# The last unit of a six-layer cross network: another product order, finals in pieces, and two quadrants transposed on TensorE in place of DMA

## The chip, the core and the metric

The kernel runs on one core of one Trainium2 chip. The metric is device time in microseconds (us), lower is better. A profile's span is some 2 us shorter than the time of its run. Because the change touches only the last 25 us of 2300, I use one more number throughout, the **tail**: from the end of the last full-size product on TensorE to the end of the span, both read from one profile (spans are given to 0.1 us, so a tail is good to some 0.05 us).

## The reference

```python
# x0: 16384 x 1024, ws: 6 x 1024 x 1024, bs: 6 x 1024, all bf16
x = x0
for l in range(6):
    proj = x @ ws[l] + bs[l]
    x = x0 * proj + x
return x
```

## The kernel before

It takes 1024 rows at a time through all six layers, with the rows along the free dimension. A *unit* is one layer for 1024 rows. In the last unit each matrix product is a Strassen-Winograd product of 2x2 blocks: seven block products P1 to P7, each of four groups (m = 0 to 3) of four 128x128x512 matmuls. They accumulate into eight banks of PSUM: `pA` and `pX`. Four quadrants of the output follow from them: Q (P1, P2), U (P1, P6, P3, P5), V (P1, P6, P7, P5) and W (P1, P6, P7, P4). ScalarE empties the banks, VectorE adds P5 where it is due, multiplies by x0 and adds x (the *finals*).

A hand-written table of ranks gives the order in which operations are issued; each engine and each DMA queue then works in that order. In the last unit the finals write a tile that a DMA transposes to row order, and a second DMA stores it. The part that matters:

```python
ttop("Ua", U[:], U[:], P5s[:], ADD, ...)          # whole quadrants, 128x2048
ttop("Va", V[:], V[:], P5s[:], ADD, ...)
for nm, C, q in (("Q", Q, (0, 0)), ("U", U, (0, 1)), ("V", V, (1, 1)), ("W", W, (1, 0))):
    ...                                            # C *= x0   (W in two halves)
    if not last: ...
    else:
        def fin(...): tt(xfin[...], v4(C[:]), v4(blk(xs, eh, n)), ADD)
        def tr(...):  nc.sync.dma_start_transpose(out=xo[...], in_=xfin[...])
        z = base + {"Q": 40, "U": 41, "V": 42, "W": 43}[nm]
        op(z, tr, ...)
        def st(...):  nc.sync.dma_start(out[...], xo[...])
        op(z + 10, st, ...)                        # all stores rank behind all transposes
```

Of the kernel before, what the change touches and what calls it, by code (L numbers as in the profile page):

```python
# [7 lines left out]

ADD = mybir.AluOpType.add
SUB = mybir.AluOpType.subtract  # L10
MULT = mybir.AluOpType.mult
BF16 = mybir.dt.bfloat16
# [4 lines left out]
def ranks(text):  # L17

    return {w.split("@")[0]: float(w.split("@")[1]) for w in text.split()}
# [25 lines left out]
""")  # L45
RFIRST = {**R0, **ranks("""
T1@-5 c5@-4.5 T2@-4 c6@-3.5 T3@-3 c7@-2.5 c3@-2 T4@-1 2i5@15 2i6@15.1 2i3@15.2 2i7@15.3 5i5@15.4 5i6@15.5 5i3@15.6 5i7@15.7
""")}
SPAN2, SPAN0 = 23.4, 24.2

# [2 lines left out]
def kernel(  # L53
# [7 lines left out]
    nc = tc.nc  # L61
    P = nc.NUM_PARTITIONS
# [3 lines left out]
    KH = KD // 2  # L66
    H = D // 2
    NB = 512
    PR = 2 * NB
    assert D == 1024 and B % PR == 0  # L70
    NPAIR = B // PR
    KQ, HQ, NQ = KH // 2, H // 2, NB // 2
# [3 lines left out]
    const = ctx.enter_context(tc.tile_pool(name="const", bufs=1))  # L76
# [8 lines left out]
    pA = [psum.tile([P, NB], FP32, name=f"pA{i}") for i in range(KH)]  # L85
    pX = [psum.tile([P, NB], FP32, name=f"pX{i}") for i in range(KH)]
    x0Ts = [work.tile([P, 2, KD, NB], BF16, name=f"x0T{i}") for i in range(2)]
    xsts = [work.tile([P, 2, KD, NB], BF16, name=f"xst{i}") for i in range(2)]
# [4 lines left out]
    P1s, P5s, Q, U, V, W = (work.tile([P, KH, NB], BF16, name=f"ev{i}") for i in range(6))  # L93
    isum = [work.tile([P, KH, H], BF16, name=f"isum{i}") for i in range(2)]
    zeros = const.tile([P, NB], BF16, name="zeros")
    LK = L * KD
    b_bf = const.tile([P, LK], BF16, name="b_bf")
    b_all = const.tile([P, LK], FP32, name="b_all")

    def blk(t, dh, n):  # L100
        return t[:, n, dh * KH:(dh + 1) * KH, :]

    def tt(o, a, b, op):
        nc.vector.tensor_tensor(out=o, in0=a, in1=b, op=op)  # L104
# [60 lines left out]
    def op(rank, fn, rd=(), wr=(), weights=()):  # L165
        for k in weights:
            uses_left[k] = uses_left.get(k, 0) + 1
        ops.append((rank, fn, tuple(rd), tuple(wr), tuple(weights)))

    base = 0.0  # L170
    QD = ((0, 0), (0, 1), (1, 0), (1, 1))
    for u, (pr, l) in enumerate(units):
        one, first, last = level1(u), u == 0, u == NU - 1
        rk = RFIRST if first else (R0 if one else R2)
        x0T, xst = x0Ts[pr % 2], xsts[pr % 2]
        xs = x0T if l == 0 else xst
        X0 = {q: f"x0.{pr % 2}.{q[0]}{q[1]}" for q in QD}
        XO = {q: f"xs.{pr % 2}.{q[0]}{q[1]}" for q in QD}
        XI = X0 if l == 0 else XO

        def add(name, fn, rd=(), wr=(), weights=(), rk=rk, base=base, u=u):
            op(base + rk[name], fn, rd, wr, [(u, w) for w in weights])

        def ttop(name, o, a, b, o_, rd, wr, **kw):
            add(name, lambda: tt(o, a, b, o_), rd, wr, **kw)
# [15 lines left out]
        if pr == 0:  # L201
# [13 lines left out]
            for X, s in (("2i", isum[0]), ("5i", isum[1])):  # L215
                a = lambda r, c, X=X, u=u: wt[(u, X[0])][:, r * KQ:(r + 1) * KQ, c * HQ:(c + 1) * HQ]
# [31 lines left out]
        A = [f"A{m}" for m in range(KH)]  # L248
        Xn = [f"X{m}" for m in range(KH)]
        if not one:  # L250
            for X, Bm, src in (("5", T[1][:], "T1"), ("2", B21, XI[1, 0])):
                q = lambda dh, n, Bm=Bm: Bm[:, dh * KQ:(dh + 1) * KQ, n * NQ:(n + 1) * NQ]
# [15 lines left out]
        if not one:  # L268
            for X, Bm, src, a, b, C in (("5", T[1][:], "T1", 0, 1, P5s), ("2", B21, XI[1, 0], 2, 3, Q)):
                q = lambda dh, n, Bm=Bm: Bm[:, dh * KQ:(dh + 1) * KQ, n * NQ:(n + 1) * NQ]  # L270
                c = lambda dh, n, C=C: C[:, dh * KQ:(dh + 1) * KQ, n * NQ:(n + 1) * NQ]
# [48 lines left out]
        allm = lambda s: [f"{s}.{m}" for m in range(KH)]  # L320
        if not one:
            ttop("Q1", Q[:], Q[:], P1s[:], ADD, allm("Q") + allm("P1s"), allm("Q"))
        ttop("Ua", U[:], U[:], P5s[:], ADD, allm("U") + allm("5c"), allm("U"))
        ttop("Va", V[:], V[:], P5s[:], ADD, allm("V") + allm("5c"), allm("V"))
        for nm, C, q in (("Q", Q, (0, 0)), ("U", U, (0, 1)), ("V", V, (1, 1)), ("W", W, (1, 0))):
            if nm == "W":
                for h, g in enumerate("ab"):
                    sl, ms = slice(h * KQ, (h + 1) * KQ), [f"W.{2 * h}", f"W.{2 * h + 1}"]
                    ttop("Wm" + g, C[:, sl], C[:, sl], blk(x0T, *q)[:, sl], MULT, ms + [X0[q]], ms)
            else:  # L330
                ttop(nm + "m", C[:], C[:], blk(x0T, *q), MULT, allm(nm) + [X0[q]], allm(nm))
            if not last:
                ttop(nm + ("a" if nm == "Q" else "x"), blk(xst, *q), C[:], blk(xs, *q), ADD, allm(nm) + [XI[q]], [XO[q]])
            else:
                xfin = xsts[1 - pr % 2][:].rearrange("r n k (j p) -> r (n k j) p", p=P).rearrange(
                    "r (e n j k) p -> r e n j k p", e=2, n=2, j=KH)
                xo = x0Ts[1 - pr % 2][:].rearrange("r n k (j p) -> r (n k j) p", p=P).rearrange(
                    "r (e n j k) p -> r e n j k p", e=2, n=2, j=KH)
                XF = [f"xs.{1 - pr % 2}.{a}{b}" for a, b in QD]
                XT = [f"x0.{1 - pr % 2}.{a}{b}" for a, b in QD]  # L340
                eh, n = q

                def fin(eh=eh, n=n, C=C, xfin=xfin, xs=xs):
                    v4 = lambda a: a.rearrange("r k (j p) -> r k j p", p=P)
                    tt(xfin[:, eh, n].rearrange("r j k p -> r k j p"), v4(C[:]), v4(blk(xs, eh, n)), ADD)
                add(nm + ("a" if nm == "Q" else "x"), fin, allm(nm) + [XI[q]] + XF, [f"xf{eh}{n}"])

                def tr(eh=eh, n=n, xfin=xfin, xo=xo):
                    nc.sync.dma_start_transpose(out=xo[:, eh, n].rearrange("p j k r -> p (j k) r"),
                                                in_=xfin[:, eh, n].rearrange("r j k p -> r (j k p)"))  # L350
                z = base + {"Q": 40, "U": 41, "V": 42, "W": 43}[nm]
                op(z, tr, [f"xf{eh}{n}"] + XT, [f"xt{eh}{n}"])

                def st(eh=eh, n=n, xo=xo, pr=pr):
                    r0 = pr * PR + n * NB
                    nc.sync.dma_start(out[r0:r0 + NB, eh * H:(eh + 1) * H].rearrange("(j p) d -> p j d", p=P),
                                      xo[:, eh, n].rearrange("p j k r -> p j (k r)"))
                op(z + 10, st, [f"xt{eh}{n}"], ["out"])

        nxt = pr + 1  # L360
        if l == (2 if pr == 0 else 0) and nxt < NPAIR:
# [21 lines left out]
    order_ctx = ctx.enter_context(tc.manual_schedule(  # L383
        engines={nc.tensor.engine, nc.scalar.engine, nc.vector.engine, nc.sync.engine, nc.gpsimd.engine}))
    nc.vector.memset(zeros[:], 0.0)
    for i in range(NDUMMY):
        nc.tensor.matmul((pX + pA)[i % (2 * KH)][:], lhsT=zeros[:, 0:P], rhs=zeros[:], start=True, stop=True, skip_group_check=True)

# [80 lines left out]
```

## Time and profile before

| | |
|---|---|
| time, median of 4 runs | 2299.64 us (2299.07 to 2301.93) |
| span of the profile | 2297.4 us |
| last full product ends | 2277.24 us |
| tail | 20.2 us |

The page's table of busy time of the kernel before: busy us, share of the span, number of instructions.

```profile
span 2297.4 us, 34637 instructions
PE 2255.7 (98%) x12674; PEld 1261.1 (55%) x12912; DVE 2079.1 (90%) x2314; ACT 1833.8 (80%) x3223; POOL 20.3 (1%) x41
```

TensorE is busy 98% of the span, so fewer waits before the last product could gain hardly anything. The timeline of the kernel before from there on, engine by engine (start us, duration us, engine, line, operation, output<-inputs, count; SPq is the queue of DMA issues, where a merged line holds several issues and the waits between them):

```profile
2272.76 4.48 PE L190 MATMUL pA<-T,wp 128*128 128x512 bf16 x20
...
2273.97 1.23 DVE L104 TENSOR_TENSOR ev<-ev,ev 128x2048 bf16<-128x2048 bf16 x1 [8.86 <-ACT ev L199]
2275.23 1.23 DVE L104 TENSOR_TENSOR ev<-ev,x0T 128x2048 bf16<-128x2048 bf16 x1
2276.37 1.22 DVE L104 TENSOR_TENSOR ev<-ev,ev 128x2048 bf16<-128x2048 bf16 x1
2277.51 1.29 DVE L104 TENSOR_TENSOR ev<-ev,x0T 128x1024 bf16<-128x1024 bf16 x2
2278.83 2.36 DVE L104 TENSOR_TENSOR xst<-ev,xst 128x2048 bf16<-128x2048 bf16 x2
2281.11 1.22 DVE L104 TENSOR_TENSOR ev<-ev,x0T 128x2048 bf16<-128x2048 bf16 x1
2282.36 1.23 DVE L104 TENSOR_TENSOR xst<-ev,xst 128x2048 bf16<-128x2048 bf16 x1
...
2265.14 23.13 SPq L349 DMA_TRANSPOSE x0T<-xst  x4
2288.36 3.88 SPq L356 DMA_DIRECT2D out_dram<-x0T  x4
```

VectorE idles 8.86 us until ScalarE has emptied all of U's banks, and then has nearly 10 us of finals to do, 6.4 us of them after TensorE has stopped. Q's transpose is issued at 2265.14, but no store is issued before 2288.36, when the fourth transpose has been issued. W's final ends at 2280.05, before U's at 2281.19, yet W's transpose stands last in the queue. The same stretch by windows, kernel before (from:to, length, busy time of each engine, granted clock of TensorE, mean busy share of the DMA engines, which can read a little over 1, GB/s):

```profile
2280.00:2282.00 2.00, 0.00 (x0) 0.00 (x0) 2.00 (x3) 0.00 (x0) 0.00 (x0) 0.50 0.00 0
2282.00:2284.00 2.00, 0.00 (x0) 0.00 (x0) 1.55 (x2) 0.00 (x0) 0.00 (x0) 0.50 0.89 168
2286.00:2288.00 2.00, 0.00 (x0) 0.00 (x0) 0.00 (x0) 0.00 (x0) 0.00 (x0) 0.50 1.14 212
2290.00:2292.00 2.00, 0.00 (x0) 0.00 (x0) 0.00 (x0) 0.00 (x0) 0.00 (x0) 0.50 1.03 350
2294.00:2296.00 2.00, 0.00 (x0) 0.00 (x0) 0.00 (x0) 0.00 (x0) 0.00 (x0) 0.50 0.99 330
2296.00:2297.40 1.40, 0.00 (x0) 0.00 (x0) 0.00 (x0) 0.00 (x0) 0.00 (x0) 0.50 0.00 0
```

From 2282.4 to 2296.0 the DMA engines are full: about 7.4 us for three transposes at some 212 GB/s, then 6.2 us for four stores of 512 KB at some 340 GB/s. Between Q's transpose, which is through by 2269, and 2282 they stand idle. This tail is late DMA work.

### The profile page before, as it was taken

The page shows a single profiled execution, that of the slowest core. Times are in us where ns is not written, and L with a number is a line of the kernel's source. Part 1 is how long each engine was busy: PE and PEld are TensorE (multiplying, and loading weights), DVE is VectorE, ACT ScalarE, POOL GpSimd, SP SyncE. Part 2 cuts the span into 40 slices and gives each one's busy share as a digit, 9 for nine tenths or more (in the row PEclk, how much of TensorE's full clock was granted, in tenths as well). Part 3 has the DMA queues.
Part 4 walks back from the last instruction along what each step waited for, and adds up shares of the span by engine and source line. Part 5 has one row for each costly group of instructions (what it writes and reads, how often), then busy time and mean ns, then how long its engine had stood idle before and what let it go on. Part 6 is the DMA issues. An engine that isn't in the chain of part 4 may idle for free.

```text
span 2297.4 us, 34637 instructions
## 1 busy us (share of the span) xinstructions
PE 2255.7 (98%) x12674; PEld 1261.1 (55%) x12912; DVE 2079.1 (90%) x2314; ACT 1833.8 (80%) x3223; POOL 20.3 (1%) x41
## 2 busy tenths in 40 slices
PE   8999999999999999999999999999999999999996
PEld 3445555555555555555555555555555555555552
DVE  6999999999999999999999999999999999999995
ACT  4668888888888887888888888888888888878884
POOL 1100000000000000000000000000000000000000
PEclk9999999999999999999999999999999999999998
DMA  9669689695977969779697796968869698796953
GB/s 296 237 244 290 226 234 281 203 317 187 252 260 217 305 209 248 263 221 286 214 274 241 227 285 202 291 223 238 281 196 298 206 253 269 209 310 197 276 181 74
DMA packets 627932, 558.06 MB, mean 243 GB/s; under 512 B 401712, under 2 KB 554288, under 8 KB 627760
## 3 DMA queue, kind: packets, MB, share of 16 engines
q1 hardware_dynamic: 622576, 536.95, 78.7%
q0 software_dynamic: 5184, 18.88, 2.1%
q8 instruction: 101, 1.65, 0.3%
q14 instruction: 71, 0.58, 0.1%
HBM read 436.21 MB, written 52.43 MB: 213 GB/s over the span
## 4 chain that ended last, share of the span: by engine, by line
PE 96%; DVE 2%; issue 1%; DMA 1%; SPq 1%; ACT 0%; DVEq 0%; ACTq 0%
PE pA L190 56%; PE pX L288 24%; PE pX L190 16%; DVE ev L104 1%; SPq L390 0%; DMA Lc<-isum 0%; DMA x0T<-in_x_dram 0%; DVE xst L104 0%; DVE wp L104 0%; DVE T L104 0%; ACT ev L199 0%; DVE isum L104 0%; SPq L397 0%; ACT pX L195 0%; DVE ti L104 0%
## 5 line engine op out<-in xcount | busy, mean ns | idle before, releaser
L190 PEld LDWEIGHTS <-wp 128*128 128x128 bf16 x7904 | 771.9, 98 | 851.1 <-issue 10.9
L190 PE MATMUL pA<-T,wp 128*128 128x512 bf16 x4468 | 1049.6, 379 | 7.3
L199 ACT ACTIVATE ev<-pA,b_all 128x512 bf16<-128x512 f32 x1124 | 706.0, 689 | 212.8 <-PE pA L190 166.0
L288 PEld LDWEIGHTS <-wp 128*128 128x128 bf16 x4984 | 486.3, 98 | 158.9 <-issue 16.9
L104 DVE TENSOR_TENSOR ev<-ev,x0T 128x2048 bf16<-128x2048 bf16 (+1 forms) x480 | 482.8, 1007 | 7.7 <-ACT ev L199 1.3
L104 DVE TENSOR_TENSOR xst<-ev,xst 128x2048 bf16<-128x2048 bf16 x320 | 391.1, 1224 | 19.4 <-DVE ev L104 0.5
L288 PE MATMUL pX<-ti,wp 128*128 128x256 bf16 x2848 | 398.1, 272 | 0.6 <-DVE ti L104 0.6
L104 DVE TENSOR_TENSOR ev<-ev,ev 128x2048 bf16<-128x2048 bf16 x281 | 343.6, 1223 | 32.8 <-ACT ev L199 15.3
L199 ACT ACTIVATE ev<-pX,b_all 128x512 bf16<-128x512 f32 x412 | 288.9, 705 | 65.2 <-PE pX L190 46.8
L190 PE MATMUL pX<-xst,wp 128*128 128x512 bf16 x1372 | 337.9, 379 | 2.2 <-DVE xst L104 1.8
L195 ACT COPY pX<-pA 128x512 f32<-128x512 f32 x412 | 256.3, 627 | 63.5 <-PE pA L190 60.8
L190 PE MATMUL pA<-xst,wp 128*128 128x512 bf16 x1203 | 302.1, 379 | 4.0
L195 ACT CAST ev<-pX 128x512 bf16<-128x512 f32 x384 | 224.6, 619 | 38.2 <-ACT ev L199 38.0
L104 DVE TENSOR_TENSOR ev<-iu,ip 128x1024 bf16<-128x1024 bf16 x178 | 122.5, 688 | 121.1 <-ACT iu L195 121.1
L195 ACT COPY pX<-pX 128x512 f32<-128x512 f32 x356 | 208.9, 587 | 8.5
L195 ACT CAST iu<-pX 128x512 bf16<-128x512 f32 x356 | 196.8, 639 | 0.3 <-PE pX L288 0.2
L104 DVE TENSOR_TENSOR T<-xst 128x2048 bf16<-128x2048 bf16 x160 | 194.9, 1218 | 0.5
L104 DVE TENSOR_TENSOR T<-xst,T 128x2048 bf16<-128x2048 bf16 x160 | 194.9, 1218 | 0.4
L288 PE MATMUL pX<-T,wp 128*128 128x256 bf16 x1068 | 160.2, 273 | 0.0
L195 ACT CAST ip<-pX 128x512 bf16<-128x512 f32 x178 | 104.8, 589 | 55.0 <-PE pX L288 55.0
L288 PE MATMUL pX<-xst,wp 128*128 128x256 bf16 x888 | 133.2, 273 | 0.0
L104 DVE TENSOR_TENSOR xst<-ev,x0T 128x2048 bf16<-128x2048 bf16 x64 | 78.2, 1223 | 1.6
(30 smaller groups left out, 614.3 us busy)
## 6 DMA issues: line engine op xcount, KB each, us to landing
wp<-Lc SPq DMA_DIRECT2D x538, 512.0 KB, 4.6
wp<-in_ws_dram SPq DMA_DIRECT2D x288, 512.0 KB, 5.3
out_dram<-x0T SPq DMA_DIRECT2D x30, 1024.0 KB, 10.1
Lc<-wp POOLq DMA_DIRECT2D x24, 512.0 KB, 6.0
Lc<-isum POOLq DMA_DIRECT2D x12, 512.0 KB, 3.6
w<-in_ws_dram SPq DMA_DIRECT2D x6, 512.0 KB, 7.7
out_dram<-x0T SPq DMA_DIRECT2D x4, 512.0 KB, 4.7
x0T<-in_x_dram SPq DMA_TRANSPOSE x34, 7.4
```

The costliest lines, as they stand in the source:

```text
L104: nc.vector.tensor_tensor(out=o, in0=a, in1=b, op=op)
L190: nc.tensor.matmul(bank[:], lhsT=wt[(u, w)][:, k, m * P:(m + 1) * P], rhs=rhs[:, k, :], start=(start and k == 0), stop=(k == KH - 1), skip ...
L195: add(name, lambda: nc.scalar.copy(out=dst, in_=src), rd, wr)
L199: add(name, lambda: nc.scalar.activation(out=dst, in_=src, func=IDENT, bias=b_all[:, c:c + 1], scale=1.0), rd, wr)
L288: nc.tensor.matmul(pX[bank][:, m * NQ:(m + 1) * NQ], lhsT=wv[:, k, m * P:(m + 1) * P], rhs=rhs[:, k, :], start=(start and m == 0 and k == ...
```

## The change

It is to start that DMA work earlier and to take two of the transposes off the DMA engines. In the last unit only:

- The products come in the order P1 P2 P5 P6 P3 P7 P4, each with its four groups in order, so that U and V are complete before the last product, P4, which only W needs.
- U's and V's finals run in halves, W's multiply in quarters.
- Q and U keep their DMA transposes; V and W are transposed on TensorE by matmuls against an identity, into PSUM banks that are free by then. For W, a matmul of x against the identity starts the bank and the one of W accumulates onto it, which is W's last add.
- ScalarE and VectorE copy the banks out; V and W leave in two stores of 256 KB each, the last on ScalarE's queue.

```diff
+RLAST = {**R0, **ranks("""            (a table of ranks for the last unit; cut)
+ ... Ua0@16.6 Um0@17.2 Ux0@17.8 Ua1@18.4 Um1@19 Ux1@19.6 Va0@20.4 Vm0@21 Vx0@21.3 Va1@21.6 Vm1@22.2 Vx1@22.8
+ ... trQ@19 stQ@24 trU@22.5 stU@26 stVa@27 stVb@27.5 stWa@28 stWb@29
+    ident = const.tile([P, P], BF16, name="ident")
...
+            for h in range(2):
+                sl = slice(h * KQ, (h + 1) * KQ)
+                for nm, C, q in (("U", U, (0, 1)), ("V", V, (1, 1))):
+                    ttop(f"{nm}a{h}", C[:, sl], C[:, sl], P5s[:, sl], ADD, ...)
+                    ttop(f"{nm}m{h}", C[:, sl], C[:, sl], blk(x0T, *q)[:, sl], MULT, ...)
+                ttop(f"Vx{h}", V[:, sl], V[:, sl], blk(xs, 1, 1)[:, sl], ADD, ...)
+                ttop(f"Ux{h}", xfin[...][:, sl], v4(U[:])[:, sl], v4(blk(xs, 0, 1))[:, sl], ADD, ...)
+            for m in range(KH):
+                ttop(f"Wm{m}", W[:, m, :], W[:, m, :], blk(x0T, 1, 0)[:, m, :], MULT, ...)
...
+            for nm, C, bank, n in (("V", V, pX, 1), ("W", W, pA, 0)):
+                for m in range(KH):
+                    def part(src, start, stop, bank=bank, m=m):
+                        for j in range(KH):
+                            nc.tensor.matmul(bank[m][:, j * P:(j + 1) * P], lhsT=src[:, m, j * P:(j + 1) * P], rhs=ident[:],
+                                             start=(start and j == 0), stop=stop, skip_group_check=True)
+                    if nm == "W":
+                        add(f"xW.{m}", lambda part=part, xs=xs: part(blk(xs, 1, 0), True, False), ...)
+                    add(f"t{nm}.{m}", lambda part=part, C=C, nm=nm: part(C, nm == "V", True), ...)
+                    # copies: V's four and W's last on ScalarE, W's other three on VectorE
+                add(f"st{nm}a", lambda st2=st2: st2(0, KQ), ...)
+                add(f"st{nm}b", lambda st2=st2, nm=nm: st2(KQ, KH, nc.sync if nm == "V" else nc.scalar), ...)
...
+    make_identity(nc, ident[:])
```

Set against the kernel before, the table of ranks is the same up to the last unit.

More of the change, by code (lines that the diff above doesn't have):

```diff
@@ L7 @@
 from concourse._compat import with_exitstack
+from concourse.masks import make_identity
 ADD = mybir.AluOpType.add
@@ L47 @@
 T1@-5 c5@-4.5 T2@-4 c6@-3.5 T3@-3 c7@-2.5 c3@-2 T4@-1 2i5@15 2i6@15.1 2i3@15.2 2i7@15.3 5i5@15.4 5i6@15.5 5i3@15.6 5i7@15.7
+""")}
+RLAST = {**R0, **ranks("""
+P6.0@10.4 P6.1@11.3 P6.2@12.1 P6.3@13 P3.0@13.9 P3.1@14.7 P3.2@15.6 P3.3@16.4 P7.0@17.3 P7.1@18.2 P7.2@19 P7.3@19.9
+P4.0@20.8 P4.1@21.6 P4.2@22.5 P4.3@23.3
+P2.0@3.5 P2.1@4.4 P2.2@5.2 P2.3@6.1 P5.0@6.9 P5.1@7.8 P5.2@8.7 P5.3@9.5 tV.0@24.4 tV.1@24.6 tV.2@24.8 tV.3@25
+xW.0@25.1 tW.0@25.2 xW.1@25.3 tW.1@25.4 xW.2@25.5 tW.2@25.6 xW.3@25.7 tW.3@26.6
+F1.0@2.8 F1.1@3.2 F1.2@3.7 F1.3@4.1 E2.0@4.6 E2.1@5.4 E2.2@6.3 E2.3@7.2 E5.0@8.3 E5.1@9.2 E5.2@10 E5.3@10.9 F.0@11.5 F.1@12.3 F.2@13.2 F.3@14.1 E3.0@15 E3.1@15.8 E3.2@16.7 E3.3@17.5 E7.0@18.4 E7.1@19.3 E7.2@20.1 E7.3@21
+E4.0@21.9 E4.1@22.7 E4.2@23.6 E4.3@24.4 cV.0@25 cV.1@25.1 cV.2@25.2 cV.3@25.3 cW.3@27
+T4@12 Qm@12.5 Qa@13.6
+Ua0@16.6 Um0@17.2 Ux0@17.8 Ua1@18.4 Um1@19 Ux1@19.6 Va0@20.4 Vm0@21 Vx0@21.3 Va1@21.6 Vm1@22.2 Vx1@22.8
+Wm0@22.9 Wm1@23.7 Wm2@24.6 Wm3@25.4 cW.0@26.3 cW.1@26.5 cW.2@26.7
+trQ@19 stQ@24 trU@22.5 stU@26 stVa@27 stVb@27.5 stWa@28 stWb@29
 """)}
@@ L173 @@
         one, first, last = level1(u), u == 0, u == NU - 1
-        rk = RFIRST if first else (R0 if one else R2)
+        rk = RFIRST if first else (RLAST if last else (R0 if one else R2))
         x0T, xst = x0Ts[pr % 2], xsts[pr % 2]
@@ L322 @@
             ttop("Q1", Q[:], Q[:], P1s[:], ADD, allm("Q") + allm("P1s"), allm("Q"))
-        ttop("Ua", U[:], U[:], P5s[:], ADD, allm("U") + allm("5c"), allm("U"))
-        ttop("Va", V[:], V[:], P5s[:], ADD, allm("V") + allm("5c"), allm("V"))
-        for nm, C, q in (("Q", Q, (0, 0)), ("U", U, (0, 1)), ("V", V, (1, 1)), ("W", W, (1, 0))):
-            if nm == "W":
-                for h, g in enumerate("ab"):
-                    sl, ms = slice(h * KQ, (h + 1) * KQ), [f"W.{2 * h}", f"W.{2 * h + 1}"]
-                    ttop("Wm" + g, C[:, sl], C[:, sl], blk(x0T, *q)[:, sl], MULT, ms + [X0[q]], ms)
-            else:
-                ttop(nm + "m", C[:], C[:], blk(x0T, *q), MULT, allm(nm) + [X0[q]], allm(nm))
-            if not last:
-                ttop(nm + ("a" if nm == "Q" else "x"), blk(xst, *q), C[:], blk(xs, *q), ADD, allm(nm) + [XI[q]], [XO[q]])
-            else:
-                xfin = xsts[1 - pr % 2][:].rearrange("r n k (j p) -> r (n k j) p", p=P).rearrange(
-                    "r (e n j k) p -> r e n j k p", e=2, n=2, j=KH)
-                xo = x0Ts[1 - pr % 2][:].rearrange("r n k (j p) -> r (n k j) p", p=P).rearrange(
-                    "r (e n j k) p -> r e n j k p", e=2, n=2, j=KH)
-                XF = [f"xs.{1 - pr % 2}.{a}{b}" for a, b in QD]
-                XT = [f"x0.{1 - pr % 2}.{a}{b}" for a, b in QD]
-                eh, n = q
-                def fin(eh=eh, n=n, C=C, xfin=xfin, xs=xs):
-                    v4 = lambda a: a.rearrange("r k (j p) -> r k j p", p=P)
-                    tt(xfin[:, eh, n].rearrange("r j k p -> r k j p"), v4(C[:]), v4(blk(xs, eh, n)), ADD)
-                add(nm + ("a" if nm == "Q" else "x"), fin, allm(nm) + [XI[q]] + XF, [f"xf{eh}{n}"])
-                def tr(eh=eh, n=n, xfin=xfin, xo=xo):
-                    nc.sync.dma_start_transpose(out=xo[:, eh, n].rearrange("p j k r -> p (j k) r"),
-                                                in_=xfin[:, eh, n].rearrange("r j k p -> r (j k p)"))
-                z = base + {"Q": 40, "U": 41, "V": 42, "W": 43}[nm]
-                op(z, tr, [f"xf{eh}{n}"] + XT, [f"xt{eh}{n}"])
-                def st(eh=eh, n=n, xo=xo, pr=pr):
-                    r0 = pr * PR + n * NB
-                    nc.sync.dma_start(out[r0:r0 + NB, eh * H:(eh + 1) * H].rearrange("(j p) d -> p j d", p=P),
-                                      xo[:, eh, n].rearrange("p j k r -> p j (k r)"))
-                op(z + 10, st, [f"xt{eh}{n}"], ["out"])
@@ new lines, with tr, st, cp @@
+        if not last:
+            ttop("Ua", U[:], U[:], P5s[:], ADD, allm("U") + allm("5c"), allm("U"))
+            ttop("Va", V[:], V[:], P5s[:], ADD, allm("V") + allm("5c"), allm("V"))
+            for nm, C, q in (("Q", Q, (0, 0)), ("U", U, (0, 1)), ("V", V, (1, 1)), ("W", W, (1, 0))):
+                if nm == "W":
+                    for h, g in enumerate("ab"):
+                        sl, ms = slice(h * KQ, (h + 1) * KQ), [f"W.{2 * h}", f"W.{2 * h + 1}"]
+                        ttop("Wm" + g, C[:, sl], C[:, sl], blk(x0T, *q)[:, sl], MULT, ms + [X0[q]], ms)
+                else:
+                    ttop(nm + "m", C[:], C[:], blk(x0T, *q), MULT, allm(nm) + [X0[q]], allm(nm))
+                ttop(nm + ("a" if nm == "Q" else "x"), blk(xst, *q), C[:], blk(xs, *q), ADD, allm(nm) + [XI[q]], [XO[q]])
+        else:
+            free = 1 - pr % 2
+            quad = lambda t: t[:].rearrange("r n k (j p) -> r (n k j) p", p=P).rearrange(
+                "r (e n j k) p -> r e n j k p", e=2, n=2, j=KH)
+            xfin, xo = quad(xsts[free]), quad(x0Ts[free])
+            XF = [f"xs.{free}.{a}{b}" for a, b in QD]
+            XT = [f"x0.{free}.{a}{b}" for a, b in QD]
+            r0 = pr * PR
+            v4 = lambda t: t.rearrange("r k (j p) -> r k j p", p=P)
+            half = lambda s, h: [f"{s}.{2 * h}", f"{s}.{2 * h + 1}"]
+            ttop("Qm", Q[:], Q[:], blk(x0T, 0, 0), MULT, allm("Q") + [X0[0, 0]], allm("Q"))
+            ttop("Qa", xfin[:, 0, 0].rearrange("r j k p -> r k j p"), v4(Q[:]), v4(blk(xs, 0, 0)), ADD,
+                 allm("Q") + [XI[0, 0]] + XF, ["xfQ0", "xfQ1"])
+            for h in range(2):
+                sl = slice(h * KQ, (h + 1) * KQ)
+                for nm, C, q in (("U", U, (0, 1)), ("V", V, (1, 1))):
+                    ms = half(nm, h)
+                    ttop(f"{nm}a{h}", C[:, sl], C[:, sl], P5s[:, sl], ADD, ms + half("5c", h), ms)
+                    ttop(f"{nm}m{h}", C[:, sl], C[:, sl], blk(x0T, *q)[:, sl], MULT, ms + [X0[q]], ms)
+                ttop(f"Vx{h}", V[:, sl], V[:, sl], blk(xs, 1, 1)[:, sl], ADD, half("V", h) + [XI[1, 1]], half("V", h))
+                ttop(f"Ux{h}", xfin[:, 0, 1].rearrange("r j k p -> r k j p")[:, sl], v4(U[:])[:, sl],
+                     v4(blk(xs, 0, 1))[:, sl], ADD, half("U", h) + [XI[0, 1]] + XF, [f"xfU{h}"])
+            for m in range(KH):
+                ttop(f"Wm{m}", W[:, m, :], W[:, m, :], blk(x0T, 1, 0)[:, m, :], MULT, [f"W.{m}", X0[1, 0]], [f"W.{m}"])
+            for nm, n in (("Q", 0), ("U", 1)):
+                def tr(n=n, xfin=xfin, xo=xo):
+                    nc.sync.dma_start_transpose(out=xo[:, 0, n].rearrange("p j k r -> p (j k) r"),
+                                                in_=xfin[:, 0, n].rearrange("r j k p -> r (j k p)"))
+                add("tr" + nm, tr, [f"xf{nm}0", f"xf{nm}1"] + XT, [f"xo{nm}"])
+                def st(n=n, xo=xo, r0=r0):
+                    nc.sync.dma_start(out[r0 + n * NB:r0 + (n + 1) * NB, 0:H].rearrange("(j p) d -> p j d", p=P),
+                                      xo[:, 0, n].rearrange("p j k r -> p j (k r)"))
+                add("st" + nm, st, [f"xo{nm}"], ["out"])
+            for nm, C, bank, n in (("V", V, pX, 1), ("W", W, pA, 0)):
+                for m in range(KH):
+                    bn = (Xn if nm == "V" else A)[m]
+                    def part(src, start, stop, bank=bank, m=m):
+                        for j in range(KH):
+                            nc.tensor.matmul(bank[m][:, j * P:(j + 1) * P], lhsT=src[:, m, j * P:(j + 1) * P], rhs=ident[:],
+                                             start=(start and j == 0), stop=stop, skip_group_check=True)
+                    if nm == "W":
+                        add(f"xW.{m}", lambda part=part, xs=xs: part(blk(xs, 1, 0), True, False), [XI[1, 0]], [bn])
+                    add(f"t{nm}.{m}", lambda part=part, C=C, nm=nm: part(C, nm == "V", True), [f"{nm}.{m}", bn], [bn])
+                    def cp(bank=bank, m=m, n=n, nm=nm, xo=xo):
+                        d, s_ = xo[:, 1, n][:, :, m, :], bank[m][:].rearrange("p (j r) -> p j r", r=P)
+                        if nm == "V" or m == 3:
+                            nc.scalar.copy(out=d, in_=s_)
+                        else:
+                            nc.vector.tensor_copy(out=d, in_=s_)
+                    add(f"c{nm}.{m}", cp, [bn] + XT, [f"xo{nm}.{m}"])
+                def st2(k0, k1, eng=nc.sync, n=n, xo=xo, r0=r0):
+                    eng.dma_start(out[r0 + n * NB:r0 + (n + 1) * NB, H + k0 * P:H + k1 * P].rearrange("(j p) d -> p j d", p=P),
+                                      xo[:, 1, n][:, :, k0:k1].rearrange("p j k r -> p j (k r)"))
+                add(f"st{nm}a", lambda st2=st2: st2(0, KQ), half(f"xo{nm}", 0), ["out"])
+                add(f"st{nm}b", lambda st2=st2, nm=nm: st2(KQ, KH, nc.sync if nm == "V" else nc.scalar), half(f"xo{nm}", 1), ["out"])
```

## The prediction

> **What bounds the kernel now.** By the page's busy table TensorE is busy 98% of the 2297.4 us span; the chain of waits is 96% TensorE. The change leaves those 2277 us alone and works on the tail. By the timeline the last product ends at about 2277.2 us; for 20 us more TensorE does nothing. VectorE runs the finals until 2283.6 us (128x2048 operations of 1.22 us). The four DMA transposes issue in order: Q at 2265.1, U at 2281.2, V at about 2283.6, W at 2285.6 (1.9 us each to issue, about 4.4 us to landing). All four stores stand behind them in the same queue: first issue 2288.4, data until about 2296.0 (stretches: about 215 GB/s in the transposes, 340 GB/s in the stores), end 2297.4.
>
> **What the change does.**
> - The 112 products stay (0.216 us each, 24.2 us). The new order P1 P2 P5 P6 P3 P7 P4 completes U and V before W. I see no new stall: ScalarE needs 0.57 to 0.69 us per bank, TensorE gives one bank per 0.86 us. The products still end at about 2277.1.
> - Finals in halves (0.69 us, pitch about 0.6); estimated from the durations above: U done at 2273.1 (before: about 2282), V at 2276.8, W's four multiplies (0.42 us, pitch 0.34) at 2278.4, because the last bank leaves ScalarE at 2278.0.
> - Two DMA transposes stay (Q, U). U issues at about 2273.1, so Q's store goes at about 2275 and U's at about 2277.5.
> - V and W leave by 48 small matmuls (128 columns, each with a weight load). This trace has 128x256 matmuls at a pitch of 0.109 us with a weight load each, so not over that; the Trainium skill, "TensorE: Matmul & The Clock Gate", section "Back-to-back issue gap", gives about 81 ns sustained at 128 columns; no run here shows it yet. Estimate: 3.9 us, ending at 2281.0 (2282.3 at the pitch of the trace).
> - Eight copies out of PSUM: ScalarE 0.6 us each (V's four 2278.0 to 2280.2), VectorE three of W's, about 0.6 us each, to 2281.2; ScalarE the last, to about 2281.9.
> - Stores of 256 KB: last issue about 2282, on ScalarE's queue. In the trace a store's data begin about 1.35 us after its issue; 0.8 us of data; so data end at about 2284.3, the span 1.4 us later.
> - The identity is made on GpSimd early, before its first needed work at 19 us; free unless it takes over 15 us.
>
> **On the critical path.** All of the gain: the last DMA issue moves from about 2291 to about 2282, and 2.1 MB of stores and three transposes no longer queue up at the end. Span about 2286 against 2297.4: 11.3 us less.
>
> **Predicted time** 2288.4 us, range 2286.3 to 2291.5. Chances: faster by over 2%: 0.005; within 2%: 0.985; slower by over 2%: 0.01. About 0.5%, as only a tail of 20 us in 2300 can shrink.
>
> **What would show it.** In the timeline, TensorE's last full product within 0.3 us of 2277.2, the small matmuls over within 5 us after; U's transpose issued near 2273; last store issued near 2282; the stretches showing stores' data already at 2276 to 2281, and ending near 2284.5.
>
> **What would make it wrong.** Small matmuls that pitch at 0.2 us or more (plus 5 us); stores of 512-byte runs slower than the 1 KB runs of before; the first transfer on ScalarE's queue starting late; a bank wanted before ScalarE emptied it (a fraction of 1 us each); the identity's GpSimd work delaying the biases that it converts at 19.6 us.

## The result and the profile after

| | before | after |
|---|---|---|
| time, median of 4 runs | 2299.64 us | 2287.80 us (2287.12 to 2289.43) |
| span of the profile | 2297.4 us | 2285.3 us |
| last full product ends | 2277.24 us | 2277.04 us |
| tail | 20.2 us | 8.26 us |

The ratio of the times is 0.9948, with a 95% interval of 0.993 to 0.9965. The gain in time, 11.8 us, is the gain of the tail, 11.9 us.

The page's busy table of the kernel after:

```profile
span 2285.3 us, 34998 instructions
PE 2270.2 (99%) x12960; PEld 1265.4 (55%) x12960; DVE 2080.7 (91%) x2324; ACT 1837.7 (80%) x3228; POOL 20.8 (1%) x43
```

(The rise of PE's busy time is mostly not real: the trace of before lacks some matmul records, 12674 against 12912 weight loads, while that of after has 12960 of both.) The timeline of the kernel after, engine by engine:

```profile
2269.97 7.07 PE L204 MATMUL pA<-T,wp 128*128 128x512 bf16 x32
2276.88 1.27 PE L389 MATMUL pX<-ident,ev 128*128 128x128 bf16 x16
2277.98 0.39 PE L389 MATMUL pA<-ident,xst 128*128 128x128 bf16 x4
2278.20 0.39 PE L389 MATMUL pA<-ident,ev 128*128 128x128 bf16 x4
...
2279.55 0.39 PE L389 MATMUL pA<-ident,ev 128*128 128x128 bf16 x4
...
2269.16 0.69 DVE L118 TENSOR_TENSOR ev<-ev,ev 128x1024 bf16<-128x1024 bf16 x1 [4.18 <-ACT ev L213]
...
2272.67 0.69 DVE L118 TENSOR_TENSOR xst<-ev,xst 128x1024 bf16<-128x1024 bf16 x1
...
2277.39 1.42 DVE L118 TENSOR_TENSOR ev<-ev,x0T 128x512 bf16<-128x512 bf16 x4
2278.73 1.88 DVE L400 CAST x0T<-pA 128x512 bf16<-128x512 f32 x3
...
2265.01 10.22 SPq L375 DMA_TRANSPOSE x0T<-xst  x2
2275.32 2.75 SPq L380 DMA_DIRECT2D out_dram<-x0T  x2
2278.75 1.94 SPq L404 DMA_DIRECT2D out_dram<-x0T  x3
...
2279.97 0.58 ACT L398 CAST x0T<-pA 128x512 bf16<-128x512 f32 x1 [0.27 <-PE pA L389]
2280.68 0.42 ACTq L404 DMA_DIRECT2D out_dram<-x0T  x1
```

VectorE starts the finals at 2269.16 rather than 2273.97, because U's first half is there; U's final ends at 2273.36, about 8 us earlier than before (2281.19). The small matmuls follow the last product without a gap. A group of four starts every 0.225 us (2277.98, 2278.20), so one matmul every 0.056 us (the *pitch*, from start to start), although the record of each lasts 0.219 us. The last store is issued at 2280.68. The windows of the kernel after:

```profile
2274.00:2276.00 2.00, 2.00 (x11) 0.87 (x9) 1.97 (x3) 1.65 (x3) 0.00 (x0) 1.00 0.79 150
2276.00:2278.00 2.00, 1.96 (x22) 1.30 (x21) 1.93 (x5) 1.65 (x4) 0.00 (x0) 1.00 1.11 286
2278.00:2280.00 2.00, 1.93 (x35) 1.76 (x32) 2.00 (x6) 1.73 (x5) 0.00 (x0) 1.00 0.97 317
2280.00:2282.00 2.00, 0.00 (x0) 0.00 (x0) 0.61 (x2) 0.55 (x1) 0.00 (x0) 1.00 1.01 283
2282.00:2284.00 2.00, 0.00 (x0) 0.00 (x0) 0.00 (x0) 0.00 (x0) 0.00 (x0) 0.91 0.97 275
2284.00:2285.30 1.30, 0.00 (x0) 0.00 (x0) 0.00 (x0) 0.00 (x0) 0.00 (x0) 0.50 0.00 0
```

The DMA engines start again at about 2274.6, under the last product, and are nearly full until about 2284.0. All the engines are done by 2281.1; after that come 2.9 us of store data and 1.3 us to the end of the span, in which no data move.

### The profile page after: what moved, and what is told of

Same layout as the page of the kernel before. It is cut to its first block, busy times and chain, and to the rows that moved or that the text cites. A ratio compares the mean times of both kernels' runs of the same rounds, so it can differ in the third digit from the quotient of the medians.

```text
span 2285.3 us, 34998 instructions
## 1 busy us (share of the span) xinstructions
PE 2270.2 (99%) x12960; PEld 1265.4 (55%) x12960; DVE 2080.7 (91%) x2324; ACT 1837.7 (80%) x3228; POOL 20.8 (1%) x43
## 4 chain that ended last, share of the span: by engine, by line
PE 97%; DVE 1%; SPq 1%; DMA 1%; ACT 0%; issue 0%; DVEq 0%
PE pA L204 57%; PE pX L302 24%; PE pX L204 16%; DVE ev L118 1%; DMA wp<-in_ws_dram 1%; SPq L440 1%; DVE xst L118 0%; ACT ev L213 0%; DVE T L118 0%; DVE wp L118 0%; SPq L447 0%; SPq L165 0%; DVE isum L118 0%; SPq L457 0%; DVE x0T L400 0%
## 5 line engine op out<-in xcount | busy, mean ns | idle before, releaser
L118 DVE TENSOR_TENSOR ev<-ev,x0T 128x2048 bf16<-128x2048 bf16 (+2 forms) x484 | 483.4, 1000 | 7.8 <-ACT ev L213 1.3
L118 DVE TENSOR_TENSOR ev<-ev,ev 128x2048 bf16<-128x2048 bf16 (+1 forms) x283 | 343.9, 1215 | 28.2 <-ACT ev L213 11.3
L204 PE MATMUL pA<-xst,wp 128*128 128x512 bf16 x1280 | 313.5, 379 | 0.0
```

What stands on the lines that cost most here:

```text
L118: nc.vector.tensor_tensor(out=o, in0=a, in1=b, op=op)
L204: nc.tensor.matmul(bank[:], lhsT=wt[(u, w)][:, k, m * P:(m + 1) * P], rhs=rhs[:, k, :], start=(start and k == 0), stop=(k == KH - 1), skip ...
```

## The experiments

Two questions were open: which part of the change brought how much, and what sets the end now. **Theory A**: before, DMA work became possible late, and each part of the change makes some of it possible earlier or takes it away. Rivals: **B**, the stores merely stood behind the transposes in one queue; **C**, the product order alone does it, and the transposes on TensorE little. For the end now: **theory E** (the prediction's sum), the end is the last issue plus a fixed latency; **theory D**, the DMA engines' backlog sets it.

All kernels gave the right result, but for the last, which is wrong. In profiles the last full product ended between 2276.8 and 2279.4 us, with the same code before the last unit; so a single time is loose by up to 2.6 us, while the tail repeats well, as the control shows. The runs below came from three chips; where the engines do the same work (c0 on one, e5, e9 and e10 on another) the time to the last issue is the changed kernel's, 3.64 or 3.65 us. The columns: tail, time from the end of the last full product to the last issue of a store, and from that issue to the end of the span, all in us (the two parts are left empty where the argument does not use them).

| kernel | tail | to last issue | issue to end | time, median us (runs) |
|---|---|---|---|---|
| before | 20.16 | 13.7 | 6.4 | 2299.64 (4) |
| after | 8.26 | 3.64 | 4.62 | 2287.80 (4) |
| c0_after_again | 8.28 | 3.65 | 4.63 | 2288.17 (1) |
| e1_store_order | 19.12 | | | 2298.24 (4) |
| e2_order_only | 14.97 | | | 2294.36 (4) |
| e8_dma_transposes | 12.99 | | | 2292.40 (4) |
| e3_old_order | 12.52 | 9.21 | 3.31 | 2291.70 (4) |
| e4_whole_finals | 9.56 | 4.81 | 4.75 | 2288.80 (1) |
| e7_x_on_vector | 9.06 | 5.48 | 3.58 | 2287.64 (1) |
| e6_v_twice | 8.27 | 4.23 | 4.04 | 2288.97 (1) |
| e5_q_store_first | 8.19 | 3.64 | 4.55 | 2289.02 (5) |
| e9_v_one_store | 8.62 | 3.64 | 4.98 | 2287.90 (5) |
| e10_no_u_v_stores | 7.39 | 3.64 | 3.75 | 2286.15 (1, wrong result) |

The runs of e1, e2, e8 and e3 stood beside a median of 2300.17 us (7 runs), those of e5 and e9 beside 2299.95 us (9 runs).

### Control: c0_after_again

The changed kernel, unedited.

> The changed kernel once more, as a control for how much the tail (end of the last full product to end of the span) moves from profile to profile: 8.3 us again, within 0.3 us.

The tail was 8.28 us. It repeats to a few hundredths.

### What each part brought

**e1_store_order**, the kernel before with another order of issues:

```diff
-                z = base + {"Q": 40, "U": 41, "V": 42, "W": 43}[nm]
-                op(z, tr, ...)
+                z, zs = {"Q": (40, 40.5), "U": (41, 42.5), "V": (42, 44), "W": (43, 45)}[nm]
+                op(base + z, tr, ...)
-                op(z + 10, st, ...)
+                op(base + zs, st, ...)
```

> The kernel before, with nothing changed but the order of issues in the one queue: Q's store goes right after Q's transpose, U's store after V's transpose, V's and W's last. Tail here means the time from the end of the last full product to the end of the span: 20.2 us before, 8.3 us after. Theory A (the tail of before is DMA work that becomes possible late: three transposes of about 2.4 us of data and stores of 1.55 us each, behind finals that end at 2283.6): only Q's store (1.55 us) can leave early, so the tail shrinks by 1.0 to 2.5 us. Rival B (most of the gain is that stores no longer stand behind transposes in the queue): the tail shrinks by 6 us or more, and the time by as much.

The tail shrank by 1.04 us and the ratio to before is 0.9992 (0.9977 to 1.0007). Rival B falls: letting the stores pass the transposes is worth about 1 us, since Q's is the only one whose data are there well before the end.

**e2_order_only**, the kernel before with the ranks of the new product order, and Ua Um Ux Va Vm Vx ahead of W's finals:

```diff
+RLAST = {**R0, **ranks(""" (the change's ranks of P, F and E)
+T4@12 Qm@12.5 Qa@13.6 Ua@18 Um@18.2 Ux@18.4 Va@22 Vm@22.2 Vx@22.4 Wma@25.2 Wmb@25.3 Wx@26.4
+""")}
-        rk = RFIRST if first else (R0 if one else R2)
+        rk = RFIRST if first else (RLAST if last else (R0 if one else R2))
```

> The kernel before with the new product order and the finals of U and V put ahead of W's, but the finals whole, four DMA transposes, four stores behind them. Theory A: U's transpose issues near 2274.5, V's near 2278, W's near 2280.5, then 6.2 us of stores that start with W's transpose still moving: data to about 2290.4, tail about 14.7 us, 5 to 6 us of the 11.9 gained. Rival C (the order is what counts, the transposes by TensorE little): tail 10 us or less.

The tail was 14.97 us: the order of products and finals alone brings 5.2 of the 11.9 us, ratio 0.9977 (0.9962 to 0.9992). Rival C falls, and the size is that of theory A.

**e8_dma_transposes**, the changed kernel with V and W transposed by DMA:

```diff
-                    (the matmuls against the identity, the copies out of PSUM, four stores of 256 KB)
+                def tr2(...): nc.sync.dma_start_transpose(out=xo[:, 1, n]..., in_=xfin[:, 1, n]...)
+                def st2(...): nc.sync.dma_start(out[..., H:D]..., xo[:, 1, n]...)
+                ttop(f"Wx{h}", xfin[:, 1, 0]...[:, sl], v4(W[:])[:, sl], v4(blk(xs, 1, 0))[:, sl], ADD, ...)
```

> The changed kernel with V and W sent through DMA transposes again (x added on VectorE, in halves), everything else kept: order, halves, Q's and U's stores before V's transpose. Theory A: W's transpose issues near 2280.3, lands near 2285.5, W's store then needs its latency and 1.5 us of data: end near 2289.8, tail about 12.7 us, 4 to 5 us more than the changed kernel. Rival C: within 1.5 us of the changed kernel (tail 8.3).

The tail was 12.99 us, 4.7 us more than after. Its issues in the timeline:

```profile
2265.89 10.18 SPq L380 DMA_TRANSPOSE x0T<-xst  x2
2276.16 2.75 SPq L385 DMA_DIRECT2D out_dram<-x0T  x2
2279.01 5.43 SPq L390 DMA_TRANSPOSE x0T<-xst  x2
2284.53 2.79 SPq L395 DMA_DIRECT2D out_dram<-x0T  x2
```

The first store of V and W is issued at 2284.53, when V's transpose has landed and W's has been issued; after the change, V's first store is issued at 2278.75. That wait and the transposes' own data are what TensorE takes away. The edit also undoes the stores in two parts and the last one on ScalarE's queue; the 4.7 us are the worth of all this together.

**e3_old_order**, the changed kernel without its ranks for P, E and F, so that those of the old table hold:

```diff
-P6.0@10.4 P6.1@11.3 P6.2@12.1 P6.3@13 P3.0@13.9 ... E4.3@24.4     (all ranks of P, E, F and F1)
```

> The changed kernel with the old product order, all else kept. Theory A: U and V complete only at about 2273.3 and 2274.5, the twelve half finals (0.68 us each) then end at 2281.6 rather than 2277.5, the last store issues near 2284.8, tail about 11.4 us, 3 us more than the changed kernel. A rival that puts all on the transposes by TensorE expects a tail within 1 us of 8.3.

The tail was 12.52 us, 1.1 us more than I expected. The sign is theory A's; for the extra the profile shows a cause that I had not thought of. The windows of this kernel:

```profile
2277.30:2279.70 2.40, 0.00 (x0) 0.00 (x0) 2.33 (x5) 0.69 (x1) 0.00 (x0) 1.00 0.38 75
2279.70:2280.50 0.80, 0.62 (x8) 0.45 (x8) 0.77 (x2) 0.32 (x1) 0.00 (x0) 1.00 1.18 216
2280.50:2281.70 1.20, 0.00 (x0) 0.00 (x0) 1.17 (x3) 0.76 (x2) 0.00 (x0) 1.00 1.14 229
2282.50:2285.90 3.40, 3.33 (x32) 3.09 (x29) 2.66 (x5) 0.84 (x3) 0.00 (x0) 0.53 0.94 293
```

With the old order TensorE has to wait for V's finals after the last product (two gaps of 2.4 and 1.2 us), and in W's small matmuls its granted clock is down to 0.53. Two starts of a group of four in the timeline of this kernel:

```profile
2284.37 0.63 PE L380 MATMUL pA<-ident,ev 128*128 128x128 bf16 x4
2284.79 0.63 PE L380 MATMUL pA<-ident,xst 128*128 128x128 bf16 x4
```

They are 0.42 us apart, about 0.107 us for one matmul, where the changed kernel has 0.056. So W's 32 small matmuls take 3.4 us instead of 1.8, and VectorE's copies then keep that pace. That this is all of the extra was not tested by itself. The Trainium skill, "TensorE: Matmul & The Clock Gate", section "Wait — 56ns, not 53.3ns?", gives 55.6 ns warm (full clock) and 106.7 ns cold (half clock) at 128 columns; both agree with these traces.

**e4_whole_finals**, the changed kernel with U's and V's finals whole:

```diff
-            for h in range(2):
-                sl = slice(h * KQ, (h + 1) * KQ)
+            for h in range(1):
+                sl = slice(0, KH)                 (and waits on all four banks)
```

> The changed kernel with U's and V's finals whole again (1.22 us operations, begun only when all four banks are out); W still in quarters. U's transpose should issue 1.05 us later (2274.4) and V's small matmuls begin near 2278.0 instead of 2276.9. If the halves are worth what they move, the tail grows by 0.7 to 1.2 us (9.0 to 9.5); if they are only decoration, less than 0.3 us.

The tail was 9.56 us: the halves are worth 1.3 us, slightly over the range. The last issue came 1.17 us later than in the changed kernel. Here too TensorE waited before the small matmuls, but once and for 1.30 us, and their pitch stayed at 0.056 us (sixteen in 0.90 us before W's began at 2279.64):

```profile
2278.74 1.07 PE L390 MATMUL pX<-ident,ev 128*128 128x128 bf16 x16 [1.30 <-DVE ev L118]
```

**e7_x_on_vector**, W's x added by VectorE:

```diff
+                ttop(f"Wx{m}", W[:, m, :], W[:, m, :], blk(xs, 1, 0)[:, m, :], ADD, ...)
-                    if nm == "W":
-                        add(f"xW.{m}", lambda part=part, xs=xs: part(blk(xs, 1, 0), True, False), ...)
-                    add(f"t{nm}.{m}", lambda part=part, C=C, nm=nm: part(C, nm == "V", True), ...)
+                    add(f"t{nm}.{m}", lambda part=part, C=C, nm=nm: part(C, True, True), ...)
```

> The changed kernel with W's x added by VectorE in four quarters (0.42 us, pitch 0.34) in place of the sixteen extra small matmuls. VectorE's finals end about 1.4 us later, and its three copies out of PSUM stand behind them; the last store issues near 2282.1 instead of 2280.7. Theory E: the tail grows by 1.2 to 1.6 us. Theory D: by 0.3 to 0.8 us, as part of the delay is taken up by the backlog of the DMA engines.

The last issue came 1.84 us later, the end only 0.80 us. So adding x on TensorE is worth 0.8 us (the upper edge of theory D's range), at 16 small matmuls (0.9 us of TensorE). That the end moves by less than half of what the last issue moves speaks for theory D.

### What sets the end now

**e6_v_twice**, V's small matmuls done twice:

```diff
-lambda part=part, C=C, nm=nm: part(C, nm == "V", True)
+lambda part=part, C=C, nm=nm: [part(C, nm == "V", True) for _ in range(2 if nm == "V" else 1)]
```

> The changed kernel with V's sixteen small matmuls done twice (the second overwrites the first): TensorE and the last copies about 0.9 us later, at the measured pitch of 0.056 us. Theory D (the end is set by the DMA engines, busy without a gap from about 2276.5 to 2284.0 with U's transpose and 2.1 MB of stores): the tail grows by less than 0.4 us. Theory E, as the prediction had it (the end is the last issue plus 1.35 us, 0.8 us of data and 1.4 us): the tail grows by 0.8 to 1.0 us.

The last issue came 0.59 us later (I had expected 0.9), and the tail stayed at 8.27 us. Theory E falls: a later last issue cost nothing here. The last issue in the timeline of this kernel, whose last product ended at 2278.53:

```profile
2282.76 0.42 ACTq L404 DMA_DIRECT2D out_dram<-x0T  x1
```

**e10_no_u_v_stores**, without the stores of U and V (wrong):

```diff
-                add("st" + nm, st, [f"xo{nm}"], ["out"])
+                if nm == "Q":
+                    add("st" + nm, st, [f"xo{nm}"], ["out"])
...
+                if nm == "V":
+                    continue
```

> The changed kernel with the last stores of U and V left out, so that its result is wrong on purpose (those rows of the output are never written): all engines do what they did, only 1 MB of store data is gone. In the changed kernel and its repeat the span ends 4.62 us after the last issue; where less stood before it (the one with x on VectorE, the one with the old order) it ended 3.6 and 3.3 us after. Theory D (the last store waits behind the backlog of U's and V's stores): the last issue stays at about 3.6 us after the last full product and the end comes 3.3 to 3.7 us later, tail 6.9 to 7.4 us instead of 8.3. Theory E (the last issue and its fixed latency set the end): tail 8.0 to 8.4 us.

The last issue stayed at 3.64 us after the last product; the end came 3.75 us after it (0.05 us over the range) in place of 4.62. The backlog of U's and V's stores is thus worth 0.87 us to the last store, which stands on another engine's queue. (In e7 and e3, where W's stores came late, the end came 3.58 and 3.31 us after the last issue, so the figure is loose by some 0.4 us.) The DMA packets say the same: those of ScalarE's queue begin at 2282.59 after the change, 1.91 us after the last issue, and here 1.12 us after it. These packets are from the trace that was kept of this kernel, which is of a second execution (span 2284.6 us): tail 7.3 us, last issue 3.64 us after the last product, the end 3.7 us after that. The windows of the first execution show the DMA engines idle, then W's two stores alone:

```profile
2279.00:2280.00 1.00, 0.91 (x17) 0.73 (x14) 1.00 (x3) 0.73 (x3) 0.00 (x0) 1.00 0.00 0
2281.00:2282.00 1.00, 0.00 (x0) 0.00 (x0) 0.00 (x0) 0.00 (x0) 0.00 (x0) 1.00 1.02 289
2282.00:2283.00 1.00, 0.00 (x0) 0.00 (x0) 0.00 (x0) 0.00 (x0) 0.00 (x0) 1.00 0.76 220
```

The Trainium skill, "DMA: Bandwidth & Descriptors", section "Issuing engines are not separate DMA queues", says that transfers run on the same 16 engines whichever engine starts them, so that a second issuing engine saves only the time of issuing. This agrees: ScalarE's own queue did not spare the last store the 0.87 us.

**e5_q_store_first**, Q's store issued ahead of U's transpose:

```diff
-trQ@19 stQ@24 trU@22.5 stU@26 stVa@27 stVb@27.5 stWa@28 stWb@29
+trQ@19 stQ@19.5 trU@22.5 stU@26 stVa@27 stVb@27.5 stWa@28 stWb@29
```

> The changed kernel with Q's store issued ahead of U's transpose in the same queue: it then leaves near 2269.5, in a stretch where the DMA engines idle, and 1.55 us of data leave the tail. Theory D (DMA engines set the end): the tail shrinks, but not by all of 1.55 us, because U's store cannot move before 2278.8: by 0.3 to 0.6 us. Theory E (the last issue sets the end): less than 0.2 us. In time 2287.4 against 2287.8, which rounds can hardly resolve; the tail in the profile decides.

The tail was 8.19 us, 0.07 us less: my number for theory D was wrong. The store did leave early (issued at 2271.71, long before U's transpose at 2275.76). The windows of this kernel show what happened in its old place:

```profile
2279.50:2280.00 0.50, 0.46 (x9) 0.29 (x7) 0.50 (x2) 0.50 (x1) 0.00 (x0) 1.00 0.01 1
2280.00:2280.50 0.50, 0.50 (x11) 0.50 (x10) 0.50 (x3) 0.50 (x3) 0.00 (x0) 1.00 0.00 0
2280.50:2281.00 0.50, 0.50 (x13) 0.50 (x11) 0.50 (x3) 0.50 (x3) 0.00 (x0) 1.00 0.08 27
2281.00:2281.50 0.50, 0.50 (x13) 0.50 (x11) 0.50 (x2) 0.50 (x3) 0.00 (x0) 1.00 1.00 346
```

U's transpose moves until 2279.5; U's store is issued at 2280.03 and its data begin only near 2281. In the changed kernel Q's store fills this hole of some 1.5 us. So theory D has to be narrowed, after the fact and with no test of its own: the backlog that sets the end is U's, V's and W's 1.57 MB, and it begins when U's transpose has landed and U's store has got under way, not with Q's. Against the kernel before the ratio was 0.995 (0.9937 to 0.9962), the same as the change's within the interval.

**e9_v_one_store**, as e5, with V in one store:

```diff
+                if nm == "V":
+                    add("stVb", lambda st2=st2: st2(0, KH), allm("xoV"), ["out"])
+                    continue
```

> As the kernel with Q's store first, and V leaves in one store of 512 KB with runs of 1 KB in place of two of 256 KB with runs of 512 bytes. If runs of 512 bytes are slower (the changed kernel moved about 280 GB/s where they ran alone, about 340 with 1 KB runs), the tail shrinks by up to 0.3 us more; if the later issue (after V's fourth copy, 1 us later) leaves the DMA engines a gap, it grows by up to 0.5 us. Against the kernel before: tail about 8 us, time about 2287.5 us.

The tail was 8.62 us: the later issue left the DMA engines another gap (share 0.49 from 2280 to 2281), and that cost more than longer runs won, if they won anything. Against the kernel before the ratio was 0.9946 (0.9932 to 0.996). No kernel beats the change by more than the noise.

## Why the prediction was right

Predicted 2288.4 us (2286.3 to 2291.5), measured 2287.8 us. Point by point:

- *"The products still end at about 2277.1."* 2277.04; no stall in the new order.
- *"U done at 2273.1"*, U's transpose then issued: the final ended at 2273.36. *V at 2276.8*: 2277.47. VectorE's halves started 0.61 to 0.73 us apart, not 0.6.
- *"All of the gain"* is the tail: yes, 11.9 us in the tail, 11.8 us in the time. The parts: 5.2 us from before to e2 (order of products and finals), 2.0 us more to e8 (halves, quarters, Q's and U's stores ahead of the later transposes), 4.7 us more to the change (transposes of V and W on TensorE, with their stores in two parts). The split depends on the sequence: taken out of the change, the order is worth 4.3 us (e3).
- *"Estimate: 3.9 us"* for the 48 small matmuls: mis-sized. They took 2.9 us, from 2276.88 to about 2279.8, W's at 0.056 us each in a row, not 0.081. With it the last issue came 3.64 us after the last product instead of 4.9.
- *"In the trace a store's data begin about 1.35 us after its issue; 0.8 us of data; ... the span 1.4 us later"*: this sum, 3.55 us, took the last store as alone. Without the backlog of U's and V's stores it is 3.75 us (e10); in the change it is 4.62 us. So what the prediction missed is the queue of bytes before the last store. This error of about +1.1 us and the one before of about -1.3 us nearly cancel, and that is luck: it is part of why the number came out so well. Inside the sum, too, two terms were off and nearly cancel: Q's store in e5, with nothing before it, began to move 0.9 us after its issue, not 1.35, and a store of 256 KB that ran alone (W's first in e7) moved for about 1.1 us, not 0.8. The prediction did list stores of 512-byte runs as a risk. (A run is the contiguous piece that a store writes of one row.) Where only such stores ran, the windows show 275 to 289 GB/s, against some 340 for 1 KB runs before; but these stores are also half as large, and the two were not varied apart.
- *The identity is free*: GpSimd's two operations lasted 0.20 and 0.29 us and were done by 1.3 us.

## What to carry to other kernels

When TensorE is busy 98% and only the end is left, work on the end as a schedule of its own: finish first the outputs with the longest way out, in pieces, so that DMA engines that idle during the last products start then. Cost the end as a queue of bytes on the DMA engines as well as a chain of latencies, and see which ends later; a shorter chain (from e6 to the change the last issue comes 0.59 us earlier) or a transfer moved out of a hole (e5) then brings nothing. Transposes on TensorE are cheap right behind the products, but watch the clock: in e3, after two gaps of 2.4 and 1.2 us, it was down to about half and their cost nearly doubled, while in e4, after one gap of 1.30 us, they still ran at full pace. Where between the two the clock falls was not measured.

## What the Trainium skill lacked or had wrong

- "TensorE: Matmul & The Clock Gate", section "Back-to-back issue gap", gives about 81 ns as sustained at 128 columns in a stream with a weight load for each matmul; here such a stream ran at 56 ns (0.225 us for four). The same page's section "Wait — 56ns, not 53.3ns?" has the right figures for both clocks (56 and 107 ns measured).
- "VectorE: DVE Perf Modes", section "The three transpose paths", gives 390 ns for a 128x128 transpose on TensorE. As the cost of one in a series that misleads: here, by ordinary matmuls against an identity, each further one in a row added 56 ns, though each record lasts 219 ns.
- "Advanced Engine Details and Errata", section "X-Bar Transpose (TRN2)", says that DMA transposes are as fast as regular ones and expects 350 to 400 GB/s. Here transposes of 512 KB within the core's memory moved at 204 to 220 GB/s, stores with 1 KB runs at some 340; a regular copy within the core's memory was not measured.
- No page that I read gives, for this chip, the rate of stores to DRAM by length of run: 256 KB stores in 512-byte runs 275 to 289 GB/s, 512 KB stores in 1 KB runs some 340.
